# Intermediate stores moved to GpSimd's DMA queue, and the activations for d W2 turned by DMA instead of TensorE

## The chip, the cores and the metric

The kernel runs on one core of one Trainium2 chip. The metric is the device time of one execution in microseconds (us), as a median over runs. A profiled execution, from which every duration below is read, is one more run with its own time.

## What is computed

A gated state-space block, forward and backward in one launch. Sequence length L is 2048, width D 512, state size N 128, hidden width F 1792, all in bf16.

```python
xn = layernorm(x)
s  = ssm_conv(xn)                       # kernel K from A, B, C, dt; FFT convolution over 2L, plus xn * Dskip
g  = silu(silu(xn @ w1) @ w2)           # the dense branch
out = x + s * g
```

The outputs are `out` and, for a given `grad_out`, the gradients of x, of the six real arrays A, B and C (real and imaginary), of log_dt, Dskip, w1 and w2. The gradient of w2 is `silu(h)^T @ d_o`, where `h = xn @ w1` and `d_o` is the gradient at the second product's output. TensorE sums over partitions, so `silu(h)` is needed there with tokens on the partitions. The forward part stores h to DRAM (`Hd`) with the hidden index on the partitions, so it has to be turned.

## The kernel before, in words

**Stages.** (1) Setup: loads, layer norm, tables of sines. (2) Up to about 250 us: `gen_ffn_fwd` runs over eight chunks of 256 tokens, and is paced against a chain of `gen_tables`, `gen_conv_x` and `gen_conv_fwd` for four blocks of 128 channels. (3) `gen_gate_rows` (silu of the dense branch and its slope, in rows) and the last `gen_conv_fwd`. (4) From about 333 to 521 us: `gen_ffn_da` over eight chunks, interleaved with `gen_conv_bwd` for four blocks and with `gen_out`. (5) To the end: `gen_ssm_bwd` (sixteen groups), interleaved with `gen_dw2` followed by `gen_dw1`, and with `gen_ln_bwd`.

**What goes through DRAM.** Stages hand tiles over in DRAM: tables `Ed` (L427) and `Yd` (L438), spectra `Ud` (L500) and `KXd` (L514), the convolution's result `Sd` (L525), the gradients `dUd` (L657), `DHd` (L879) and `Pd` (L888). All of these are stored from the SyncE queue. The hidden `Hd` (L553), `Od` (L563) and the outputs are stored from the GpSimd queue through `k.st`, which is `nc.gpsimd.dma_start`. Nearly all loads, and all turned loads (`dma_start_transpose`), are issued from SyncE; a few small transfers (`Kd`, `dKd`) are issued from ScalarE.

**Names for the steps.** `Kb` (L509) is the convolution kernel read back from `Kd`; `dft_fwd` multiplies by the first DFT matrix (L284), turns the result by DMA (`dB<-dA`, L287), and multiplies by the second (L296, L297); `spectrum_in` (L491) loads a spectrum as `sp_in`; `dft_inv` goes back (L309, L318). `S_b` (L522) is one block of the convolution's result, and `gate_s` (L596) multiplies the gate's `do` by it. `W2T` (L1076) and `W1T` (L857) are the turned weights for the backward products `ps_da` (L874) and `ps_dx` (L885). `doT` (L854) is `do` turned, `slope` (L864) is a load of `Hd`, and `dhT` (L876) is the gradient at h, stored as `DHd`. In the last stage, `load_params` (L345) loads six turned arrays `par_*`; `ssm_fold` loads `GE` (L667) and sums it on TensorE (L683, L685) into `Gf`; `ssm_turned` loads `YT` turned (L705) and `ssm_half` loads `Eb` (L698); `ssm_v` (L716) makes `ps_v`, copied by ScalarE to `Vb`; VectorE multiplies (`Tp`, L726); `ssm_sums` (L738 to L743) adds up `psS` on TensorE. `gen_dw1` loads `dh_tok` turned from `DHd` (L930) and multiplies it with `xn` in blocks of sixteen matmuls (L935). `gen_ln_bwd` loads `du`, `Gt` and `pd_l` (L948, L950, L952).

**d W2.** `gen_dw2` runs over fourteen blocks `ft` of 128 hidden columns. `load(ft)` reads `Hd[ft]` plainly, in rows of 4 KB, into `h_in` (two buffers). `turned` makes sixteen transposes of 128x128 on TensorE into two PSUM tiles, and ScalarE reads each of them through silu into `a_tok` (two buffers). Sixteen matmuls (L917) with `do` follow. Loads run two blocks ahead of the matmuls, turns one block ahead. `gen_dw2` yields sixteen times in all, two of them before its loop.

**What sets the order.** The generators are interleaved by hand-written weights (the last line of the kernel: `[2, 1, 1]`), and a scheduler then sets the order of instructions on each engine and each queue. A queue issues in order: what stands behind a waiting DMA waits too. A tile that takes the place of an earlier one waits for that one's last user.

Of the kernel before, what the change touches and what calls it, by code (L numbers as in the profile page):

```python
# [9 lines left out]
ACT = mybir.ActivationFunctionType  # L10
# [6 lines left out]
P = 128  # L17
# [86 lines left out]
def slope_less_one(nc, u, t):  # L104
# [1 line left out]
    nc.vector.tensor_scalar(out=t, in0=t, scalar1=-0.5, scalar2=0.5, op0=ALU.mult, op1=ALU.add)  # L106
    nc.vector.tensor_single_scalar(out=u, in_=u, scalar=-1.0, op=ALU.add)
    nc.vector.tensor_tensor(out=u, in0=u, in1=t, op=ALU.mult)


def turned(k, src, n, out, ev):

    for i in range(0, n, 8):
        pt = k.pf.tile([P, 8, P], BF16, name="pt_t", tag="pf")
        for j in range(8):
            k.nc.tensor.transpose(out=pt[:, j], in_=src(i + j), identity=k.ident[:])
        ev(out[:, i:i + 8], pt[:])


def run(gen):  # L120
# [275 lines left out]
def gen_tables(k, b):  # L396
# [5 lines left out]
    for h in range(2):  # L402
        hs = slice(b * P + 64 * h, b * P + 64 * h + 64)
        mag = tbl.tile([P, NX, 64], BF16, name="mag", tag="mag")
        nc.sync.dma_start(mag[:].rearrange("p e d -> p (e d)"), k.Md[2 * b + h])
        E = tbl.tile([P, 2, 16, NE, 4], BF16, name="E", tag="E", bufs=2)
        Y = k.Y[h]
        H = tbl.tile([P, 2, 16, 3, 4], BF16, name="H", tag="H")
        qe = lambda ap: ap.rearrange("p e (q a) -> p e q a", a=4)
        for (x0, n) in ((0, 8), (8, 8), (16, 5), (21, 7), (28, 3)):  # L410
            V = tbl.tile([P, 2, 8, 64], I32, name="V", tag="tv", bufs=2)
            TS = nc.vector.tensor_single_scalar
            TT(out=V[:, 1, 0:n], in0=k.tau[:, hs].unsqueeze(1).to_broadcast([P, n, 64]),
               in1=k.ecst[:, x0:x0 + n].unsqueeze(2).to_broadcast([P, n, 64]), op=ALU.mult)
            TS(out=V[:, 0, 0:n], in_=V[:, 1, 0:n], scalar=-float(1 << (PB - 2)), op=ALU.add)
            TS(out=V[:, :, 0:n], in_=V[:, :, 0:n], scalar=32 - PB, op=ALU.logical_shift_left)
            sn = tbl.tile([P, 2, 8, 64], BF16, name="sn", tag="ts", bufs=2)
            nc.scalar.activation(out=sn[:, :, 0:n], in_=V[:, :, 0:n], func=ACT.Sin, scale=-2 * PI_LO / 2.0 ** 32)
            for c in range(2):
                if x0 < NE:  # L420
                    segs = [(E[:, c, :, x0:x0 + n, :], 0, n)]
                else:
                    segs = [(Y[:, c, :, 1:8, :] if x0 == NE else H[:, c], 0, n)]
                for o, s0, s1 in segs:
                    TT(out=o.rearrange("p q e a -> p e q a"), in0=qe(sn[:, c, s0:s1]), in1=qe(mag[:, x0 + s0:x0 + s1, :]), op=ALU.mult)
            yield
        nc.sync.dma_start(k.Ed[b, h], E[:].rearrange("p c q e a -> p (c q e a)"))  # L427
        lo = lambda c: Y[:, c, :, 0:8, :].unsqueeze(2).to_broadcast([P, 16, 3, 8, 4])
        hi = lambda c: H[:, c].unsqueeze(3).to_broadcast([P, 16, 3, 8, 4])
        out = lambda c: Y[:, c, :, 8:32, :].rearrange("p q (k m) a -> p q k m a", m=8)  # L430
        shp = [P, 16, 3, 8, 4]
        for c, (x, y), op in ((0, ((0, 0), (1, 1)), ALU.subtract), (1, ((0, 1), (1, 0)), ALU.add)):
            m1 = tbl.tile(shp, BF16, name="m1", tag="tv", bufs=2)
            m2 = tbl.tile(shp, BF16, name="m2", tag="tm", bufs=1)
            TT(out=m1[:], in0=lo(x[0]), in1=hi(x[1]), op=ALU.mult)
            TT(out=m2[:], in0=lo(y[0]), in1=hi(y[1]), op=ALU.mult)
            TT(out=out(c), in0=m1[:], in1=m2[:], op=op)  # L437
        nc.sync.dma_start(k.Yd[b, h], Y[:].rearrange("p c q j a -> p (c q j a)"))  # L438
        yield
        for q0 in range(0, 16, 8):  # L440
            W = tbl.tile([P, 4, 8, NE, 4], BF16, name="W", tag="W", bufs=2)
            for m, (cm, ec) in enumerate(((0, 0), (1, 1), (2, 1), (1, 0))):
                d0 = hs.start + 4 * q0
                ct = k.CT[:, cm, d0:d0 + 32].rearrange("p (q a) -> p q a", a=4).unsqueeze(2).to_broadcast([P, 8, NE, 4])
                TT(out=W[:, m], in0=E[:, ec, q0:q0 + 8], in1=ct, op=ALU.mult)
            for u in range(2):
                ps = k.pt.tile([P, 4, 84], F32, name="ps_k", tag="pt")
                for q in range(4):
                    for m in range(4):
                        nc.tensor.matmul(out=ps[:, q], lhsT=Y[:, m // 2, q0 + 4 * u + q].rearrange("p j a -> p (j a)"),  # L450
                                         rhs=W[:, m, 4 * u + q].rearrange("p e a -> p (e a)"), start=(m == 0), stop=(m == 3))
                qq = 16 * h + q0 + 4 * u
                k.evk(Xr[:, :, :, qq:qq + 4], ps[:].rearrange("p q (e a) -> p a e q", a=4))
            yield
# [40 lines left out]
def gen_conv_x(k, b):  # L495

    bs = slice(b * P, b * P + P)
    dft = k.dft
    U, _ = yield from dft_fwd(k, dft, lambda t: k.xn[:, t, bs], k.evc)
    k.nc.sync.dma_start(k.Ud[b], U[:].rearrange("p c g k -> p (c g k)"))  # L500
    yield


def gen_conv_fwd(k, b):

    nc, dft = k.nc, k.dft
    bs = slice(b * P, b * P + P)
    Kb = dft.tile([P, 4, 16, 32], BF16, name="Kb", tag="t4")
    nc.sync.dma_start(Kb[:].rearrange("p a t q -> p a (t q)"), k.Kd[b].rearrange("a i (r s) x -> (i r) a (s x)", s=2))  # L509
    for _ in range(LAG):  # L510
        yield
    KX, A2 = yield from dft_fwd(k, dft, lambda t: Kb[:, :, t, :], k.evc)
    U = spectrum_in(k, dft, b, "U")
    nc.sync.dma_start(k.KXd[b], KX[:].rearrange("p c g k -> p (c g k)"))  # L514
    yield
    cplx_mul(k, dft, KX, U)
    S = dft.tile([P, 16, P], BF16, name="S_b", tag="t4")

    def consume(t0, n, ps):
        xd = dft.tile([P, 8, P], BF16, name="xd", tag="cm2")  # L520
        nc.vector.tensor_tensor(out=xd[:], in0=k.xn[:, t0:t0 + n, bs], in1=k.Dbc[:, bs].unsqueeze(1).to_broadcast([P, n, P]), op=ALU.mult)
        nc.vector.tensor_tensor(out=S[:, t0:t0 + n], in0=ps[:], in1=xd[:], op=ALU.add)  # L522
    yield from dft_inv(k, A2, U, k.evc, consume)
    k.S_b = S
    nc.sync.dma_start(k.Sd[b], S[:].rearrange("p t d -> p (t d)"))  # L525
    yield


# [98 lines left out]
def gen_conv_bwd(k, b):  # L627
# [26 lines left out]
        TT(out=xd[:], in0=k.ds[:, t0:t0 + n, bs], in1=k.Dbc[:, bs].unsqueeze(1).to_broadcast([P, n, P]), op=ALU.mult)  # L654
        TT(out=du[:, t0:t0 + n], in0=ps[:], in1=xd[:], op=ALU.add)
    yield from dft_inv(k, A2, KX, k.evc, consume_dx)
    nc.sync.dma_start(k.dUd[b], du[:].rearrange("p t d -> p (t d)"))  # L657
    yield


# [187 lines left out]
def gen_ffn_da(k, da):  # L848
# [3 lines left out]
    for c in range(T // 2):  # L852
# [6 lines left out]
        for f in range(FT // 2):  # L859
# [16 lines left out]
            nc.vector.scalar_tensor_tensor(out=dh[:, i0:i0 + 2, :], in0=dh[:, i0:i0 + 2, :], scalar=1.0, in1=ps[:], op0=ALU.add, op1=ALU.mult)  # L876
            if f in (3, 6):
                f0, n = (0, 8) if f == 3 else (8, 6)
                nc.sync.dma_start(k.DHd[f0:f0 + n, :, 256 * c:256 * c + 256].rearrange("f p n -> p f n"), dh[:, 0:n])  # L879
            yield  # L880
        for t in range(2):
            pd = da.tile([P, D], BF16, name="pd_s", tag="pd_s", bufs=1)
            ps = k.pf.tile([P, D], F32, name="ps_dx", tag="pf")
            for ft in range(FT):
                nc.tensor.matmul(out=ps[:], lhsT=dhs[ft // 8][:, ft % 8, t * P:t * P + P], rhs=k.W1T[:, ft, :],  # L885
                                 start=(ft == 0), stop=(ft == FT - 1))
            k.evb(pd[:], ps[:])
            nc.sync.dma_start(k.Pd[:, 2 * c + t, :], pd[:])  # L888
            yield


def gen_dw2(k, fw):
    nc = k.nc

    def load(ft):
        h = fw.tile([P, k.T, P], BF16, name="h_in", tag="h_in", bufs=2)
        nc.sync.dma_start(h[:].rearrange("p t n -> p (t n)"), k.Hd[ft])
        return h

    def turn(h):  # L900
        a = fw.tile([P, k.T, P], BF16, name="a_tok", tag="a_tok", bufs=2)
        turned(k, lambda t: h[:, t], k.T, a, lambda out, in_: nc.scalar.activation(out=out, in_=in_, func=ACT.Silu))
        return a
    h = load(0)
    yield
    a = turn(h)
    h = load(1)
    yield
    for ft in range(k.FT):
        at = a  # L910
        if ft + 1 < k.FT:
            a = turn(h)
            if ft + 2 < k.FT:
                h = load(ft + 2)
        ps = k.pf.tile([P, k.D], F32, name="ps_w2", tag="pf")
        for t in range(k.T):
            nc.tensor.matmul(out=ps[:], lhsT=at[:, t, :], rhs=k.do[:, t, :], start=(t == 0), stop=(t == k.T - 1))  # L917
        ob = fw.tile([P, k.D], BF16, name="o11", tag="o11", bufs=2)
        k.evb(ob[:], ps[:])
        k.st(k.outs[11][ft * P:ft * P + P, :], ob[:])  # L920
        yield
# [197 lines left out]
```

## Time and profile before

| | |
|---|---|
| median of 3 runs | 766.86 us (765.82 to 766.95) |
| profiled execution: time, span | 765.82 us, 764.0 us |
| mean granted TensorE clock | 0.906 |
| busy PE / PE load / DVE / ACT / POOL | 591.7 / 421.9 / 545.3 / 494.8 / 88.7 us |
| SyncE's DMA queue (q1) | 143.94 MB, 73.2% of the 16 DMA engines |
| GpSimd's DMA queue (q0) | 18.10 MB, 7.0% |
| packets under 512 B | 159921 of 234993 |

How to read the profile: PE is TensorE's matmul stream and PEld its weight loads, which overlap; DVE is VectorE, ACT is ScalarE, POOL is GpSimd, SP is SyncE. "SPq" marks the issue of a DMA on SyncE's queue. The rows of slices cut the span into 40 equal parts and give the busy share in tenths. In a line of waits stand the waiting instruction, what ended the wait, and the total us, count and longest. In a line of the timeline stand start, duration (us), engine, source line, operation, output and input. In a line of stretches stand the stretch, its length, the busy us and count of PE, PE load, DVE, ACT and POOL, then granted clock, DMA share and GB/s.

### The profile page before, as it was taken

How to read it: one execution, taken by the hardware profiler on the slowest of the kernel's cores; microseconds unless marked ns; L12 is line 12 of the kernel's file. 1: busy time of each engine (PE TensorE's matmuls, PEld its weight loads, DVE VectorE, ACT ScalarE, POOL GpSimd, SP SyncE). 2: the span in 40 equal slices, each digit the busy share in tenths (PEclk: the TensorE clock that was granted, in tenths of full speed). 3: DMA queues.
4: the chain of work that ended last, by engine and by line, in shares of the span. 5: the costliest groups of instructions: out<-in, count | busy, mean ns of one | idle time of the engine just before them, and what ended most of it. 6: DMA issues, size and time to landing. Idle time of an engine off the chain costs nothing. (4 is left out here: it accounts for less than half of the span.)

```text
span 764.0 us, 13488 instructions
## 1 busy us (share of the span) xinstructions
PE 591.7 (77%) x5260; PEld 421.9 (55%) x5260; DVE 545.3 (71%) x1110; ACT 494.8 (65%) x692; POOL 88.7 (12%) x167
## 2 busy tenths in 40 slices
PE   0479977898998615668898798993599878899885
PEld 0336663675764413356575475771566646678775
DVE  6979988685987985796786696980353975998500
ACT  5869767788898655475785687740476768864111
POOL 2020110011010352000000000000000013031130
PEclk9979988999999866889999899997599998999998
DMA  9989978499689759999969979235899999766492
GB/s 258 345 174 270 250 220 240 170 248 274 236 215 307 297 166 227 288 296 302 231 211 249 242 220 236 80 114 128 208 217 270 235 312 243 209 139 108 79 189 56
DMA packets 234993, 167.36 MB, mean 219 GB/s; under 512 B 159921, under 2 KB 213169, under 8 KB 231089
## 3 DMA queue, kind: packets, MB, share of 16 engines
q1 hardware_dynamic: 221952, 143.94, 73.2%
q0 software_dynamic: 6224, 18.10, 7.0%
q10 hardware_dynamic: 6752, 4.46, 2.0%
q8 instruction: 41, 0.67, 0.4%
q14 instruction: 24, 0.19, 0.1%
HBM read 65.40 MB, written 62.26 MB: 167 GB/s over the span
## 5 line engine op out<-in xcount | busy, mean ns | idle before, releaser
L42 ACT CAST dA<-ps_s 128x1024 bf16<-128x1024 f32 x96 | 94.3, 1029 | 37.5 <-PE ps_s L297 22.5
L546 PE MATMUL ps_h<-XT,W 128*128 128x256 bf16 x448 | 61.2, 288 | 32.9 <-DMA XT<-xn 26.5
L546 PEld LDWEIGHTS <-W 128*128 128x128 bf16 x448 | 45.4, 103 | 43.4 <-issue 19.6
L726 DVE TENSOR_TENSOR Tp<-Vb,Eb 128x1344 bf16<-128x1344 bf16 x64 | 52.5, 853 | 22.8 <-ACT Vb L42 13.3
L309 PE MATMUL ps_i<-I,sp_in 128*128 128x256 bf16 x384 | 55.9, 296 | 13.6 <-DVE sp_in L332 8.7
L42 ACT CAST dB<-ps_i 128x1024 bf16<-128x1024 f32 x48 | 47.2, 1020 | 29.2 <-PE ps_i L309 23.5
L559 PE MATMUL ps_o<-W,aT 128*128 128x512 bf16 x224 | 58.5, 400 | 3.2 <-ACT aT L552 1.8
L296 PE MATMUL ps_s<-dB,F 128*128 128x512 bf16 x96 | 41.0, 427 | 23.3 <-DMA dB<-dA 20.4
L874 PE MATMUL ps_da<-doT,W2T 128*128 128x256 bf16 x448 | 54.8, 276 | 0.5 <-DVE dhT L876 0.5
L309 PEld LDWEIGHTS <-sp_in 128*128 128x128 bf16 x384 | 38.6, 105 | 29.4 <-DVE sp_in L332 12.6
L935 PE MATMUL ps_w<-dh_tok,xn 128*128 128x256 bf16 x448 | 53.0, 273 | 1.6 <-DMA dh_tok<-DHd 1.6
L885 PE MATMUL ps_dx<-W1T,dhT 128*128 128x512 bf16 x224 | 53.7, 379 | 0.7 <-DVE dhT L876 0.7
L917 PE MATMUL ps_w<-do,a_tok 128*128 128x512 bf16 x224 | 53.9, 390 | 0.0
L874 PEld LDWEIGHTS <-W2T 128*128 128x128 bf16 x448 | 44.2, 99 | 9.3 <-issue 2.5
L42 ACT CAST o<-ps_w 128x256 bf16<-128x256 f32 (+1 forms) x42 | 18.6, 442 | 45.8 <-PE ps_w L935 34.6
L42 ACT CAST Vb<-ps_v 128x672 bf16<-128x672 f32 x64 | 42.6, 723 | 8.7 <-PE ps_v L716 7.3
L935 PEld LDWEIGHTS <-xn 128*128 128x128 bf16 x448 | 42.8, 98 | 7.3 <-issue 2.8
L876 DVE SCALAR_TENSOR_TENSOR dhT<-dhT,ps_da 128x512 bf16<-128x512 bf16 x56 | 37.2, 682 | 12.3 <-PE ps_da L874 11.7
L284 PEld LDWEIGHTS <-TF 128*128 128x128 bf16 x384 | 26.3, 103 | 32.6 <-DMA Kb<-Kd 16.3
L297 PE MATMUL ps_s<-dB,F 128*128 128x512 bf16 x96 | 41.0, 427 | 0.0
L450 PE MATMUL ps_k<-W,Y 128*128 128x84 bf16 x512 | 28.5, 212 | 13.3 <-DVE Y L437 10.2
L450 PEld LDWEIGHTS <-Y 128*128 128x128 bf16 x512 | 25.6, 105 | 23.7 <-DVE Y L437 12.9
(220 smaller groups left out, 1327.1 us busy)
## 6 DMA issues: line engine op xcount, KB each, us to landing
Yd<-Y SPq DMA_DIRECT2D x8, 1024.0 KB, 6.4
sp_in<-Ud SPq DMA_DIRECT2D x8, 1024.0 KB, 7.2
h_in<-Hd SPq DMA_DIRECT2D x14, 512.0 KB, 5.2
Ed<-E SPq DMA_DIRECT2D x8, 672.0 KB, 4.8
Eb<-Ed SPq DMA_DIRECT2D x8, 672.0 KB, 6.1
Hd<-hT POOLq DMA_DIRECT2D x8, 512.0 KB, 6.8
Ud<-dA SPq DMA_DIRECT2D x4, 1024.0 KB, 7.9
KXd<-dA SPq DMA_DIRECT2D x4, 1024.0 KB, 6.1
```

The lines of the kernel that those rows point to most:

```text
L42: return self.nc.scalar.copy(out=out, in_=in_)
L296: nc.tensor.matmul(out=ps[:, 4 * u:4 * u + 4], lhsT=F2[:, m0], rhs=B[:, 0, g0:g0 + 4, :], start=True, stop=False)
L297: nc.tensor.matmul(out=ps[:, 4 * u:4 * u + 4], lhsT=F2[:, m1], rhs=B[:, 1, g0:g0 + 4, :], start=False, stop=True)
L309: nc.tensor.matmul(out=ps[:, g], lhsT=Y[:, c, g0 + g, :], rhs=k.I2[:, c].rearrange("p c m -> p (c m)"), start=(c == 0), stop=(c == 1))
L450: nc.tensor.matmul(out=ps[:, q], lhsT=Y[:, m // 2, q0 + 4 * u + q].rearrange("p j a -> p (j a)"), rhs=W[:, m, 4 * u + q].rearrange("p e a ...
L546: nc.tensor.matmul(out=ps[:, j], lhsT=k.W1[:, dk, ft * P:ft * P + P], rhs=XTv[:, :, dk, :], start=(dk == 0), stop=(dk == DK - 1))
L559: nc.tensor.matmul(out=ps[:], lhsT=aT[:, ft, t * P:t * P + P], rhs=k.W2[:, ft, :], start=(ft == 0), stop=(ft == FT - 1))
L726: k.nc.vector.tensor_tensor(out=Tp[:, c, :, r ^ c].rearrange("p e (q w) a -> p q w e a", w=2), in0=Vb[:, :, c].rearrange("p q w (e a) -> p ...
L874: nc.tensor.matmul(out=ps[:, j], lhsT=W2T[:, dk, ft * P:ft * P + P], rhs=dTv[:, :, dk, :], start=(dk == 0), stop=(dk == DK - 1))
L885: nc.tensor.matmul(out=ps[:], lhsT=dhs[ft // 8][:, ft % 8, t * P:t * P + P], rhs=k.W1T[:, ft, :], start=(ft == 0), stop=(ft == FT - 1))
L917: nc.tensor.matmul(out=ps[:], lhsT=at[:, t, :], rhs=k.do[:, t, :], start=(t == 0), stop=(t == k.T - 1))
L935: nc.tensor.matmul(out=ps[:], lhsT=k.xn[:, t, dk * P:dk * P + P], rhs=dh[:, t].rearrange("p j n -> p (j n)"), start=(t == 0), stop=(t == k ...
```

## The change

Two things change. Eight lines that stored `Ed`, `Yd`, `Ud`, `KXd`, `Sd`, `dUd`, `DHd` and `Pd` through `nc.sync.dma_start` call `k.st` instead, so that these 64 DMAs are issued from GpSimd's queue. And `gen_dw2` loads `Hd[ft]` with a turning DMA straight into `a_tok` and applies silu there in place, in one ScalarE instruction of 128x2048; `turned`, `load` and `h_in` go away, as do the two yields before the loop. The scheduler then sets a new order on all engines.

```diff
-        nc.sync.dma_start(k.Ed[b, h], E[:].rearrange("p c q e a -> p (c q e a)"))
+        k.st(k.Ed[b, h], E[:].rearrange("p c q e a -> p (c q e a)"))
...
-        nc.sync.dma_start(k.Yd[b, h], Y[:].rearrange("p c q j a -> p (c q j a)"))
+        k.st(k.Yd[b, h], Y[:].rearrange("p c q j a -> p (c q j a)"))
...
-    k.nc.sync.dma_start(k.Ud[b], U[:].rearrange("p c g k -> p (c g k)"))
+    k.st(k.Ud[b], U[:].rearrange("p c g k -> p (c g k)"))
...
-    nc.sync.dma_start(k.KXd[b], KX[:].rearrange("p c g k -> p (c g k)"))
+    k.st(k.KXd[b], KX[:].rearrange("p c g k -> p (c g k)"))
...
-    nc.sync.dma_start(k.Sd[b], S[:].rearrange("p t d -> p (t d)"))
+    k.st(k.Sd[b], S[:].rearrange("p t d -> p (t d)"))
...
-    nc.sync.dma_start(k.dUd[b], du[:].rearrange("p t d -> p (t d)"))
+    k.st(k.dUd[b], du[:].rearrange("p t d -> p (t d)"))
...
-                nc.sync.dma_start(k.DHd[f0:f0 + n, :, 256 * c:256 * c + 256].rearrange("f p n -> p f n"), dh[:, 0:n])
+                k.st(k.DHd[f0:f0 + n, :, 256 * c:256 * c + 256].rearrange("f p n -> p f n"), dh[:, 0:n])
...
-            nc.sync.dma_start(k.Pd[:, 2 * c + t, :], pd[:])
+            k.st(k.Pd[:, 2 * c + t, :], pd[:])
...
 def gen_dw2(k, fw):
     nc = k.nc
-
-    def load(ft):
-        h = fw.tile([P, k.T, P], BF16, name="h_in", tag="h_in", bufs=2)
-        nc.sync.dma_start(h[:].rearrange("p t n -> p (t n)"), k.Hd[ft])
-        return h
-
-    def turn(h):
+    for ft in range(k.FT):
         a = fw.tile([P, k.T, P], BF16, name="a_tok", tag="a_tok", bufs=2)
-        turned(k, lambda t: h[:, t], k.T, a, lambda out, in_: nc.scalar.activation(out=out, in_=in_, func=ACT.Silu))
-        return a
-    h = load(0)
-    yield
-    a = turn(h)
-    h = load(1)
-    yield
-    for ft in range(k.FT):
-        at = a
-        if ft + 1 < k.FT:
-            a = turn(h)
-            if ft + 2 < k.FT:
-                h = load(ft + 2)
+        nc.sync.dma_start_transpose(a[:], k.Hd[ft])
+        nc.scalar.activation(out=a[:], in_=a[:], func=ACT.Silu)
         ps = k.pf.tile([P, k.D], F32, name="ps_w2", tag="pf")
         for t in range(k.T):
-            nc.tensor.matmul(out=ps[:], lhsT=at[:, t, :], rhs=k.do[:, t, :], start=(t == 0), stop=(t == k.T - 1))
+            nc.tensor.matmul(out=ps[:], lhsT=a[:, t, :], rhs=k.do[:, t, :], start=(t == 0), stop=(t == k.T - 1))
```

More of the change, by code (lines that the diff above doesn't have):

```diff
@@ L108, in slope_less_one @@
     nc.vector.tensor_tensor(out=u, in0=u, in1=t, op=ALU.mult)
[L111 to L117, printed above, removed]
 def run(gen):
```

## The prediction

> **What bounds the kernel now.** I read the 40 slices first, then busy times by stage, the SyncE queue in order of time, and single tiles. In the slices, PE and DMA share the load and no engine is full everywhere.
>
> ```profile
> PE   0479977898998615668898798993599878899885
> DMA  9989978499689759999969979235899999766492
> ```
>
> Two holes in PE stand out: at 269 to 285 us, and at 522 to 546 us. The longest PE waits name them:
>
> ```profile
> PE ps_s L284 <- DMA Kb<-Kd: 16.2, 1, 16.2
> PE G L683 <- DMA GE<-dKd: 14.7, 1, 14.7
> ```
>
> The SyncE queue tells why the first is long. The load of Kb (L509) stands behind a store of S_b that waits for VectorE until 275.85 and a load of G that waits until 279.43:
>
> ```profile
> 269.29 0.33 SPq L575 DMA_DIRECT2D G<-in_grad_out_dram  x1
> 275.85 0.33 SPq L525 DMA_DIRECT2D Sd<-S_b  x1
> 279.43 0.33 SPq L575 DMA_DIRECT2D G<-in_grad_out_dram  x1
> 279.93 0.38 SPq L509 DMA_DIRECT2D Kb<-Kd  x1
> 280.41 10.13 SPq L1076 DMA_TRANSPOSE W2T<-in_B_w_dram  x4
> 291.73 6.40 SPq L287 DMA_TRANSPOSE dB<-dA  x1
> ```
>
> The second hole is the chain par, GE, fold: the queue reaches the six parameter loads at 522.74, and GE, behind them, at 530.45:
>
> ```profile
> 522.74 1.17 SPq L345 DMA_TRANSPOSE par_Ar<-in_A_A_re_dram  x1
> 530.45 2.66 SPq L667 DMA_DIRECT2D GE<-dKd  x4
> ```
>
> The d W2 stage (first load of h_in at 541.9 to the last at 645.9) shows busy us of PE, PE load, DVE, ACT, POOL, then clock and DMA share:
>
> ```profile
> 541.90:645.90 104.00, 88.22 (x876) 63.89 (x877) 65.52 (x149) 72.89 (x115) 11.28 (x21) 0.90 1.02 252
> 716.00:757.00 41.00, 36.18 (x325) 30.66 (x323) 10.14 (x39) 8.14 (x21) 7.13 (x12) 1.00 0.67 136
> ```
>
> A DMA share of 1.02 over 104 us (packets of one engine overlap, so it can pass 1) says that the DMA engines pace it, with PE (85%) close. From 716 only d W1 is left and PE runs through: 20 blocks of 16 matmuls by 755.9, 2.02 us each; 8.1 us of last store and end follow.
>
> **What the Trainium skill says.** "DMA: Bandwidth & Descriptors", section "Issuing engines are not separate DMA queues", says that all issuers share the same 16 DMA engines and another issuer saves sequencer time only. The trace fits: a 512 KB store from GpSimd (Hd) lands in 6.8 us, a load of that size from SyncE (slope) in 5.1. "SBUF — State Buffer", section "SBUF: two separate sides", warns that VectorE's fast modes can keep GpSimd from writing descriptors. Here all 16 Hd issues took 828 to 2342 ns, median 864, beside a VectorE over 80% busy: no such block to speak of. "Advanced Engine Details and Errata", section "X-Bar Transpose (TRN2)", calls turned DMAs as fast as plain ones. This trace disagrees: turned loads move in packets of 256 B at 25 ns on average, plain 4 KB rows in packets at 202 ns (packet records), so 512 KB takes 2048 x 25 / 16 = 3.2 us of all 16 engines against 128 x 202 / 16 = 1.6 us.
>
> **The change part by part.** The sum is against the profiled execution, 765.82 us (span 764.0), and stands 1.04 us below the median of 766.86.
>
> *1. Stores to GpSimd.* 64 issues leave SyncE: 8 Ed, 8 Yd, 4 each of Ud, KXd, Sd and dUd, 16 DHd, 16 Pd. A SyncE issue is about 0.35 us, 64 x 0.35 = 22 us of a queue that is not full; GpSimd gains 64 x 0.6 = 38 us and was busy 12%. Cost in bytes: none. Up to 250 us the built order differs little, and the turned loads dB start when their data is ready, not behind a store: 0, with +-4 for the new order. On GpSimd stores now stand among the gate's tensor_scalars, but VectorE needs S_b there in the same order: 0.
>
> *2. 269 to 366 us.* Kd lands about 274.5, the store and the fourth G load no longer stand before Kb: it goes at 274.5 instead of 279.9, a gain of 5.5 us. But in the built order W1T (issue 11.7 us in this trace, 8.7 at best) now stands before both dB, and W2T before it. From 274.5: four W2T, 9 to 10 us; G, S, S, 1.5; W1T, 10 to 11; so dB goes at 297 where it now goes at 291.7, and lands at 305.5 (now 299.9). The U load for the same product comes after the second dB: issue 309, landing 315.5 (now 304.85). The first ps_da, now at 333.3, then starts near 338: +5. W1T is out of the way and the slopes are ready by then, which takes back about 2 of the PE gaps of 2.9 and 3.6 us at 338 and 351: net +3.
>
> *3. 366 to 521 us.* Loads no longer wait behind DHd, Pd and dUd, whose waits on SyncE sum to 20.8, 22.8 and 10.8 us; but PE itself waits only 5.9 us (418 us), 2.6 and 2.8 for dB here. I take back 3, bounds 0 and 8.
>
> *4. The boundary.* SyncE's order is now: two a_tok, eight loads of the layer norm's backward and three dh_tok, all ahead of par and GE. The first dh_tok waits for the last DHd store of the first eight rows (VectorE at 514.5, landing near 519), each takes 2.4 to 3 us of issue, and loads of du, Gt and pd_l between them wait for buffers until about 525. So par goes at 529 instead of 522.7: +6.5 for GE. PE fills the hole with two d W2 blocks (32 x 0.213 = 6.8 us). The first ps_v, which now stands after the h_in wait (landing 546), comes at 543.7 + 6.5 = 550.2, not 546.5.
>
> *5. d W2.* Removed: 224 turns on PE, 0.059 us apart in the rows of 16, 13.2 us; 28 ScalarE silus x 1.03 = 28.9 us, replaced by 14 of 128x2048, 1.92 each (row dhT L865) = 26.9 us. Added: 14 turned loads for 14 plain ones, (3.2 - 1.6) x 14 = 22 us of the 16 engines.
>
> ```profile
> L897 SPq DMA_DIRECT2D h_in<-Hd x14: 319/512/977, 541.9 to 645.9; - x14
> L930 SPq DMA_TRANSPOSE dh_tok<-DHd x14: 1317/3008/6394, 594.7 to 742.5; - x14
> h_in<-Hd SPq DMA_DIRECT2D x14, 512.0 KB, 5.2
> dh_tok<-DHd SPq DMA_TRANSPOSE x14, 6.5
> ```
>
> (The first two: issue time in ns, least, median, most; the others: us to landing.) Two a_tok, three dh_tok and eight loads left the stage (part 4). Packets of 537 to 646 sum to 112 us over 16; by the same prices, Eb 11, YT 36, GE 7, twelve a_tok 39, one dh_tok 3, eleven small loads 10, stores 12, scaled by 112/117, the new stage has 113. It starts at 543, four later. The old depth, two h_in and two a_tok, shrinks to two a_tok, each loaded only after the matmuls of two blocks before: I take 1.00 instead of 1.03 of the engines. The last a_tok goes at 656; 8 us landing (dh_tok: 5.1 to 10.2), 1.9 silu, 4.5 wait and matmuls end d W2 at 670.4. The third block starts near 567, after the fourth ps_v as the built order has it, so a pair of blocks takes (670.4 - 567) / 6 = 17.2 us.
>
> *6. The tail.* At that point the order leaves eight groups of psS (2.4 us), six of ps_v (1.15), ten d W1 blocks (1.75) and the rest, 44.4 us of PE work; the old stretch from 672.5 to 715.5 took 1.19 times its work: 52.8 us. Then 18 d W1 blocks, not 20: 36.4 us, and 8.1. End: 670.4 + 97.3 = 767.7 of span, +3.7.
>
> Sum: +3 - 3 + 3.7 = +3.7, 769.5 profiled, **770.5** as a median.
>
> **The rivals.** Everything hangs on the pair's time p: the end moves by 6p - 99.7 us, break-even p = 16.6.
> *Faster:* the d W2 stage is paced by PE, not by DMA. Then the 13.2 us of turns and 6.8 us put in the hole count in full. p = 15 gives 6 x 15 - 99.7 = -9.7, 757. For it: PE 19.6 of 20 us at 560 to 600; floor of p: 6.5 landing + 1.9 + 3.6 = 12. Against: the share of 1.02 to 1.08. It decides below 16.6.
> *Much slower:* the loop of load, silu and matmul holds SyncE, with YT queued behind an a_tok that waits for PE, and ScalarE, where Vb stands behind a silu that waits for DMA. p = 20 gives +20, 787. For it: SyncE and ScalarE keep their order; against: the two loads of a pair overlap.
> *Nothing to be seen:* stores change the queue's name only, 112 against 113 us of packets, p near 16.6: 767.
>
> **How the numbers follow.** The likeliest, +1.5 to +12: 0.38; much slower: 0.17; faster: 0.34; nothing: 0.11. A measurement here tells 0.2% (1.5 us) from no change. Slower is 0.38 + 0.17 = 0.55. The range reaches from p near 14.2, 752, to p near 20.2, 788; the likeliest's own is 768 to 779.
>
> **What would show it.** Kb issued near 274 and the first dB near 297; ps_da first near 338; par near 529; two d W2 blocks at 522; last d W2 matmul near 670; DMA share near 1.0 in the stage; 18 d W1 blocks after the last psS. If the last d W2 matmul comes before 660, I am wrong towards faster; if ScalarE stands long before the a_tok silus, towards slower.

## The result, and the profile after

The changed kernel takes 791.49 us (median of 4, 790.96 to 794.53), the kernel before 766.34 beside it: a ratio of 1.0352, 95% interval 1.0299 to 1.0405, so 3 to 4% slower. The forecast was 770.5, and the time lies above its range of 752 to 788. The profiled execution of the changed kernel took 790.96 us, span 789.2 (before 764.0): 25.2 us to be found. Beside the experiments the kernel before has medians of 760 to 764, so from here on ratios are compared. In the tables below "us" is the median of all runs, while the ratio leaves out runs more than 1.5% above their kernel's fastest, as the profiled executions of e1, e3, e13 and e14 were, so that for e1, e3 and e14 the traces of their repetitions e16, e18 and e17 are read, and of e13 only the order at the boundary. All points in time are those of one profiled execution.

The slices, from the page of the changed kernel:

```profile
PE   0589876897988623478799398899178866799887
DMA  9997868599479789988849949568899989958564
```

The hole at 270 us has become shallower and longer (2, 3, 4 from 276 to 335 us), a new one (3) stands at 434 to 454 us, and that at the boundary is deeper (1). From the waits of PE: who waited, for what, total us, times, longest.

```profile
PE ps_s L287 <- DMA dB<-dA: 36.8, 7, 12.6
PE ps_s L275 <- ACT dA L42: 16.9, 5, 8.2
PE G L674 <- DMA GE<-dKd: 16.6, 1, 16.6
PE ps_s L275 <- DMA Kb<-Kd: 7.4, 1, 7.4
```

As forecast, the wait for Kb has shrunk (16.2 before) and that for GE has not. The wait for dB has grown from 20.4 us to 36.8, that for ScalarE's dA from 6.4 to 16.9. The two lines of before:

```profile
PE ps_s L296 <- DMA dB<-dA: 20.4, 7, 5.9
PE ps_s L284 <- ACT dA L42: 6.4, 6, 5.2
```

SyncE's queue, in order of time:

```profile
276.74 0.33 SPq L566 DMA_DIRECT2D G<-in_grad_out_dram  x1
277.24 0.38 SPq L500 DMA_DIRECT2D Kb<-Kd  x1
277.79 10.89 SPq L1050 DMA_TRANSPOSE W2T<-in_B_w_dram  x4
292.94 0.33 SPq L566 DMA_DIRECT2D G<-in_grad_out_dram  x1
293.32 0.91 SPq L593 DMA_DIRECT2D S<-Sd  x2
294.27 9.69 SPq L848 DMA_TRANSPOSE W1T<-in_B_w_dram  x1
304.07 10.03 SPq L278 DMA_TRANSPOSE dB<-dA  x2
...
519.09 7.61 SPq L887 DMA_TRANSPOSE a_tok<-Hd  x2
532.52 0.37 SPq L922 DMA_DIRECT2D du<-dUd  x1
...
542.78 2.07 SPq L904 DMA_TRANSPOSE dh_tok<-DHd  x1
...
545.53 3.52 SPq L904 DMA_TRANSPOSE dh_tok<-DHd  x1
...
550.68 3.56 SPq L904 DMA_TRANSPOSE dh_tok<-DHd  x1
554.29 1.28 SPq L336 DMA_TRANSPOSE par_Ar<-in_A_A_re_dram  x1
...
562.17 2.65 SPq L658 DMA_DIRECT2D GE<-dKd  x4
```

Two things are to be seen. W1T stands before both dB, which go at 304.07 (before 291.73); and the fourth G load stands behind the four W2T, at 292.94 (before 279.43, ahead of them). At the boundary par stands behind loads that wait for stores to land: du for the last dUd store (landed 532.38), the first dh_tok for a DHd store (landed 542.65). SyncE stands for 5.8 and 7.4 us there, with par behind. The two stores on GpSimd, with GpSimd's own wait in brackets:

```profile
529.43 0.56 POOL L648 DMA_DIRECT2D dUd<-du_b  x1 [3.49 <-DVE du_b L646]
537.15 0.90 POOL L870 DMA_DIRECT2D DHd<-dhT  x1 [2.24 <-DVE dhT L867]
```

The last stage, first a_tok load behind the boundary to the last, and then d W1 alone (busy us of PE, PE load, DVE, ACT, POOL; clock, DMA share):

```profile
584.86:676.68 91.82, 70.46 (x593) 45.13 (x591) 48.44 (x110) 57.27 (x77) 9.61 (x18) 0.91 0.97 200
747.50:783.80 36.30, 33.00 (x297) 27.84 (x294) 10.12 (x39) 7.34 (x19) 6.79 (x11) 1.00 0.57 122
```

The queues and landings (the rows of q1 and q0: packets, MB, share of 16 engines; the others: size, us to landing):

```profile
q1 hardware_dynamic: 227552, 108.03, 60.3%
q0 software_dynamic: 13648, 54.01, 19.7%
...
a_tok<-Hd SPq DMA_TRANSPOSE x14, 6.9
```

Where the 25 us came from, as ends of the same work in us (par: issue):

| | before | after | later by |
|---|---|---|---|
| forward stage, last ps_o | 241.3 | 248.4 | 7.1 |
| last S_b | 322.4 | 342.9 | 20.5 |
| last ps_dx | 521.6 | 544.3 | 22.7 |
| par_Ar goes | 522.7 | 554.3 | 31.6 |
| first G | 541.4 | 572.9 | 31.5 |
| last d W2 matmul | 672.5 | 693.8 | 21.3 |
| last psS | 715.6 | 747.5 | 31.9 |
| last d W1 matmul | 755.9 | 783.8 | 27.9 |

So 22.7 us are there before the last stage begins, 8.8 come at the boundary, and what follows takes back 6.3.

### The profile page after: what moved, and what is told of

Its sections match the earlier page's. It is cut to its first block, busy times and chain, and to the rows that moved or that the text cites. A ratio compares the mean times of both kernels' runs of the same rounds, so it can differ in the third digit from the quotient of the medians.

```text
span 789.2 us, 13075 instructions
## 1 busy us (share of the span) xinstructions
PE 587.1 (74%) x5036; PEld 408.0 (52%) x5036; DVE 547.1 (69%) x1110; ACT 493.3 (63%) x678; POOL 129.4 (16%) x231
## 3 DMA queue, kind: packets, MB, share of 16 engines
q1 hardware_dynamic: 227552, 108.03, 60.3%
q0 software_dynamic: 13648, 54.01, 19.7%
## 4 chain that ended last, share of the span: by engine, by line
issue 29%; DVE 18%; DMA 18%; PE 17%; ACT 7%; POOL 6%; SPq 4%; POOLq 0%; ACTq 0%; DVEq 0%
DMA dB<-dA 4%; DMA a_tok<-Hd 4%; PE ps_dx L876 3%; DVE Tp L717 2%; PE ps_w L891 2%; DMA G<-in_grad_out_dram 2%; PE ps_i L300 2%; PE ps_da L865 2%; SPq L904 1%; POOL Hd L544 1%; DMA slope<-Hd 1%; PE ps_o L550 1%; DMA Od<-ob 1%; DMA out_dram<-go_x 1%; DVE g_t L751 1%
## 5 line engine op out<-in xcount | busy, mean ns | idle before, releaser
L42 ACT CAST dA<-ps_s 128x1024 bf16<-128x1024 f32 x96 | 94.5, 1028 | 56.2 <-PE ps_s L288 40.4
L287 PE MATMUL ps_s<-dB,F 128*128 128x512 bf16 x96 | 42.2, 440 | 39.5 <-DMA dB<-dA 36.8
L891 PE MATMUL ps_w<-do,a_tok 128*128 128x512 bf16 x224 | 57.4, 408 | 16.7 <-ACT a_tok L888 16.7
L42 ACT CAST dB<-ps_i 128x1024 bf16<-128x1024 f32 x48 | 47.3, 1024 | 24.4 <-PE ps_i L300 20.2
L909 PE MATMUL ps_w<-dh_tok,xn 128*128 128x256 bf16 x448 | 53.7, 273 | 1.2 <-DMA dh_tok<-DHd 0.7
L320 DVE TENSOR_TENSOR cm<-sp_in,dA 128x1024 bf16<-128x1024 bf16 x24 | 16.5, 689 | 47.8 <-ACT dA L42 31.8
L891 PEld LDWEIGHTS <-a_tok 128*128 128x128 bf16 x224 | 22.1, 103 | 43.8 <-ACT a_tok L888 18.2
L42 ACT CAST o<-ps_w 128x256 bf16<-128x256 f32 (+1 forms) x42 | 18.5, 439 | 40.9 <-PE ps_w L909 32.3
L888 ACT ACTIVATE a_tok<-a_tok 128x2048 bf16<-128x2048 bf16 x14 | 26.6, 1910 | 27.1 <-DMA a_tok<-Hd 27.1
L288 PE MATMUL ps_s<-dB,F 128*128 128x512 bf16 x96 | 41.6, 433 | 0.0
```

Source lines behind the costliest of these rows:

```text
L42: return self.nc.scalar.copy(out=out, in_=in_)
L287: nc.tensor.matmul(out=ps[:, 4 * u:4 * u + 4], lhsT=F2[:, m0], rhs=B[:, 0, g0:g0 + 4, :], start=True, stop=False)
L288: nc.tensor.matmul(out=ps[:, 4 * u:4 * u + 4], lhsT=F2[:, m1], rhs=B[:, 1, g0:g0 + 4, :], start=False, stop=True)
L891: nc.tensor.matmul(out=ps[:], lhsT=a[:, t, :], rhs=k.do[:, t, :], start=(t == 0), stop=(t == k.T - 1))
L909: nc.tensor.matmul(out=ps[:], lhsT=k.xn[:, t, dk * P:dk * P + P], rhs=dh[:, t].rearrange("p j n -> p (j n)"), start=(t == 0), stop=(t == k ...
```

## Experiments

### One part at a time: e1 to e4, e16, e18

e1 has all 64 stores on GpSimd and the old d W2; e2 the new d W2 and the old stores; e3 only the forward stores (Ed, Yd, Ud, KXd, Sd); e4 only the backward stores (dUd, DHd, Pd). e16 and e18 are e1 and e3 once more. The edit of e4, for one of its three lines:

```diff
-            nc.sync.dma_start(k.Pd[:, 2 * c + t, :], pd[:])
+            k.st(k.Pd[:, 2 * c + t, :], pd[:])
```

> All eight kinds of store (64 DMAs) from GpSimd's queue, d W2 as before. Theory A, drawn from the trace after: the moved stores alone, by the order that the scheduler then builds, cost nearly everything: the last ps_dx ends near 544 (before 521.6), and the time is 785 to 791. Theory B, the prediction on record: moved stores cost nothing up to the boundary: last ps_dx within 4 us of 521.6, time 763 to 770.

> Only d W2 changed (turned by DMA, silu in place); all stores from SyncE as before. Theory A: up to 521 us nothing moves (the built order is the same until there), and the d W2 stage and its tail cost +2 to +6: 768 to 773. Rival (much slower loop, p near 20): 785 to 790. Rival (PE-paced, p 15): near 757.

> Only the five forward stores (Ed, Yd, Ud, KXd, Sd; 28 DMAs) from GpSimd, d W2 as before. In its built order W1T already stands before both dB of the last forward convolution. Theory A (the order of loads in the forward part and in the last convolution is the cause): most of the +22, 780 to 788, first ps_da chunk ends near 358. Theory C (each issue on GpSimd costs its share, whichever it is): 28/64 of +22, near 776. Theory B: 763 to 770.

> Only the three backward stores (dUd, DHd, Pd; 36 DMAs) from GpSimd, d W2 as before; W1T stays behind both dB in its built order. Theory A: little, 763 to 770, first ps_da chunk near 349. Theory C (each issue on GpSimd costs its share): 36/64 of +22, near 779.

> The kernel of e1 once more, since the profiled execution of e1 was the longest of its 20 runs (779.5 us against a median of 770.4). Theory A: the order is the same, so the last S_b comes again near 341 and the last ps_dx 530 to 544; par goes 16 to 18 us ahead of the last ps_dx, as with backward stores alone; time 765 to 773. Rival (a part of the delay in e1's profile was chance): S_b below 335.

> The kernel of e3 once more, since its profiled execution was among the longer of its runs. Theory A: the last S_b again near 342 and Kb near 277, since both follow from the order; time 771 to 779. Rival: S_b below 335.

| | us | ratio to before (95%) | last ps_o | last S_b | last ps_dx | par goes | first G |
|---|---|---|---|---|---|---|---|
| e1 | 770.4 | 1.0063 (1.0030 to 1.0097) | | | | | |
| e16 | 764.4, one run | before 762.6 | 246.7 | 341.5 | 540.2 | 523.8 | 546.3 |
| e2 | 766.9 | 1.0042 (1.0015 to 1.0069) | 241.8 | 320.9 | 519.7 | 530.4 | 550.2 |
| e3 | 776.4 | 1.0143 (1.0111 to 1.0176) | | | | | |
| e18 | 778.2, one run | before 762.6 | 246.7 | 342.1 | 535.6 | 536.6 | 555.2 |
| e4 | 747.2 | 0.9782 (0.9719 to 0.9844) | 240.9 | 321.3 | 521.4 | 504.6 | 527.3 |

The delay of the forward stage and of S_b belongs to the forward stores: e18 has it whole, e4 and e2 not at all. Theory C (a price for each issue on GpSimd) falls with e4: 36 of the 64 issues, and no delay. Theory A was wrong on the times of e1, e3 and e4: e3's 776.4 is the figure of theory C, below A's 780 to 788, and e4 gains 2.2%, at the boundary. e2 came out near the lower end of its theory A: 2.8 us above the kernel before, expected +2 to +6. The timeline of SyncE in e4:

```profile
495.46 0.36 SPq L864 DMA_DIRECT2D slope<-Hd  x1
504.60 1.16 SPq L345 DMA_TRANSPOSE par_Ar<-in_A_A_re_dram  x1
...
512.61 2.66 SPq L667 DMA_DIRECT2D GE<-dKd  x4
```

Before, nine stores that wait for VectorE and ScalarE stand between the slope load at 499.59 and par at 522.74. With these on GpSimd, par goes 16.8 us ahead of the last ps_dx, and the first G ends 5.9 us behind it instead of 19.8. e16 shows the same (16.4 and 6.1), and so e1 pays back most of its forward loss.

The two parts don't add up: e1 and e2 alone lose 0.6% and 0.4%, together 3.5%. What the stores gain at the boundary is missing in the changed kernel, where par goes 10.0 us behind the last ps_dx. Nor do the two groups of stores add up: the forward ones cost 1.4% alone (e3), 2.9% where the backward ones are moved as well (e1 against e4, 1.0063 / 0.9782), and 3.5% in the changed kernel (1.0352 / 1.0006, e7 below). One place where they meet can be seen. PE's longest wait for dB between 400 and 460 us is 5.9 us before, 4.5 in e4 and 6.2 in e18, but 10.2 in e16 and 12.6 in the changed kernel. No run takes that wait out by itself, so how much of the difference it makes is open.

### The boundary: e6, e7, e8, e13, e15

e7 is the changed kernel with the forward stores back on SyncE. e6 is the changed kernel, and e13 is e7, with the first du, pd_l and dh_tok made to wait for par, so that par and GE go first; e15 is e13 with a third a_tok buffer. e8 joins e6 to the edit of e5 below. Each copy makes the load behind it wait:

```diff
+    k.p1c = par["Ci"][:, 0:1]
...
+        if c < 2:
+            nc.gpsimd.tensor_copy(du[:, 0, 0, 0:1], k.p1c)
         nc.sync.dma_start(du[:].rearrange("p b t d -> p b (t d)"), k.dUd[:, :, 256 * c:256 * c + 256].rearrange("b p n -> p b n"))
...
+        if c < 2:
+            nc.gpsimd.tensor_copy(pd[:, 0, 0:1], k.p1c)
         nc.sync.dma_start(pd[:], k.Pd[:, 2 * c:2 * c + 2, :])
...
+            if f < 2:
+                nc.gpsimd.tensor_copy(dh[:, 0, j, 0:1], k.p1c)
             nc.sync.dma_start_transpose(dh[:, :, j, :], k.DHd[2 * f + j])
```

```diff
-        a = fw.tile([P, k.T, P], BF16, name="a_tok", tag="a_tok", bufs=2)
+        a = fw.tile([P, k.T, P], BF16, name="a_tok", tag="a_tok", bufs=3)
```

> The changed kernel, but the first loads of du, pd_l and dh_tok made to wait for the last par load (one column of par is copied into their tiles ahead of the load), so that par and GE go out before them. Theory A (par stands behind loads that wait for stores to land, and the gain that backward stores alone had is lost there): par goes at 527 to 530 instead of 554, first G ends near 551 (changed kernel 572.6), and the time falls by 15 to 22: 769 to 776. Rival (the last stage is paced by the DMA engines, so an earlier G is given back in the d W2 stage): first G as above but time 784 to 790.

> The changed kernel, but the five forward stores back on SyncE: backward stores on GpSimd and d W2 turned by DMA. Theory A (the two parts work against each other at the boundary: the turned loads bring du and dh_tok ahead of par, where they wait for stores): the 17 us that backward stores alone gained are lost, first G near 550, time 766 to 772. Rival (the parts add up: -17 and +3): 748 to 753.

> The changed kernel with both edits: W1T behind both dB, and par and GE ahead of du, pd_l and dh_tok. Theory A: the two gains add, 755 to 763, the +7 of the forward stage remains in it. Rival (one shared limit, the DMA engines or PE, takes one of the two back): 768 to 776.

> As e7 (backward stores on GpSimd, d W2 turned by DMA), with par and GE ahead of the first du, pd_l and dh_tok, as in e6. Theory A (turning by DMA costs nothing by itself; its price is the place of par in the queue): par goes near 505, first G ends near 530 with two d W2 blocks ahead of it, and the time falls from e7's ratio of 1.00 to about 0.98, as with backward stores alone. Rival (the turned loads and their silu slow the d W2 stage itself, so an earlier G is given back there): par near 505 but ratio 0.995 to 1.005.

> As e13, with a third buffer for a_tok. Theory A (with two buffers each load waits for the matmuls of two blocks before, and PE for load and silu: gaps of 3 to 8 us ahead of a_tok blocks): these gaps shrink and the time falls by 3 to 8 us below e13. Rival (the DMA engines pace the stage): within 3 us of e13, or slower since more turned loads stand ahead of YT.

| | us | ratio to before (95%) | par against last ps_dx | first G behind last ps_dx |
|---|---|---|---|---|
| before | | 1 | +1.1 | 19.8 |
| after | 791.5 | 1.0352 (1.0299 to 1.0405) | +10.0 | 28.6 |
| e7 | 760.6 | 1.0006 (0.9980 to 1.0031) | +10.8 | 29.5 |
| e6 | 772.7 | 1.0172 (1.0077 to 1.0268) | -17.9 | 10.5 |
| e8 | 769.5 | 1.0111 (1.0034 to 1.0189) | -18.5 | 10.5 |
| e13 | 750.2 | 0.9847 (0.9817 to 0.9877) | -17.7 | 10.5 |
| e15 | 746.6 | 0.9820 (0.9758 to 0.9882) | -16.8 | 5.9 |

From the timeline of e7: the first dh_tok waits, and par stands behind the third.

```profile
509.50 0.38 SPq L926 DMA_DIRECT2D pd_l<-Pd  x1
517.45 1.36 SPq L904 DMA_TRANSPOSE dh_tok<-DHd  x1
...
525.27 4.28 SPq L904 DMA_TRANSPOSE dh_tok<-DHd  x1
529.59 1.26 SPq L336 DMA_TRANSPOSE par_Ar<-in_A_A_re_dram  x1
```

From the timeline of e6, where nothing that waits for a store is left ahead of par:

```profile
521.90 7.96 SPq L888 DMA_TRANSPOSE a_tok<-Hd  x2
529.91 1.05 SPq L929 DMA_DIRECT2D Gt<-in_grad_out_dram  x2
531.05 1.15 SPq L336 DMA_TRANSPOSE par_Ar<-in_A_A_re_dram  x1
```

Theory A holds for e6 and e13, and for e7 by the ratio; the 760.6 us of e7 lie between the two ranges, since the kernel before stood at 760.1 there. Had the parts been additive, e7 would have had 0.9782 x 1.0042 = 0.982; it has 1.0006. With par first it has 0.985 (e13): of the 2.2 points that e7 lost against e4, 1.6 come back. The rest, 0.65 points, isn't clear of the two intervals, which overlap. So most of the price of the turned load was par's place in the queue, and what it costs as such can't be told from nothing here. The rival of e6 (an earlier G given back in the d W2 stage) falls by the median, which drops by 1.8 points of the ratio. G came at 559.5 and not at 551, since in that execution (780.5 us, the longest of e6's four) the last ps_dx ended at 549.0; part is given back, though: G is 13.4 us earlier than in the changed kernel, the last d W1 matmul 10.5. Its PE waits:

```profile
PE ps_w L892 <- ACT a_tok L889: 25.6, 9, 7.0
```

and that of e15, with three buffers:

```profile
PE ps_w L892 <- ACT a_tok L889: 4.9, 3, 2.5
```

The wait for load and silu is real, 25.6 us in e6, and with a third buffer it is 4.9 (e15). The buffer isn't shown to be the cause, though, for it changed the order as well. The first a_tok loads of e13 (first line) stand ahead of par, at 507.33; those of e15 (second line) stand behind par, at 502.19, and behind GE and four YT:

```profile
498.60 5.29 SPq L888 DMA_TRANSPOSE a_tok<-Hd  x2
523.61 5.42 SPq L888 DMA_TRANSPOSE a_tok<-Hd  x2
```

In time e15 and e13 aren't told apart: their intervals overlap. e8 has 1.0111, where the sum of both gains would give 1.0352 - 0.0133 (e5) - 0.0180 (e6) = 1.0039. That is just inside its interval, but its 769.5 us lie in the range of the rival (768 to 776) and not in that of theory A (755 to 763): whether the two gains add in full is not shown.

### The last convolution and the forward stage: e5, e9, e10, e11, e14, e17

e5 is the changed kernel with W1T made to wait for the first half of the last S_b; e9 adds a third buffer for G, so that its fourth load needn't wait:

```diff
+            nc.gpsimd.tensor_copy(k.W1T[:, 0, 0:1], k.S_b[:, 0, 0:1])
             nc.sync.dma_start_transpose(k.W1T[:], k.ins["B_w1"])
```

```diff
-        G = gp.tile([P, 4, k.D], BF16, name="G", tag="G", bufs=2)
+        G = gp.tile([P, 4, k.D], BF16, name="G", tag="G", bufs=3)
```

e10 is the kernel before with only Ed and Yd on GpSimd, e11 with only Ud, KXd and Sd (lines as in e4). e14 is the changed kernel with the edits of e5, e9 and e6, and Ed and Yd back on SyncE; e17 is e14 once more.

> The changed kernel, but the load of W1T made to wait for the first half of the last S_b (one column of S_b is copied into W1T ahead of the load), so that both dB of the last forward convolution go out before it. Theory A (W1T ahead of dB costs stage 3): the last S_b comes near 329 to 331 (changed kernel 342.9, before 322.4; the rest of the delay is there before W1T), and all later points 11 to 14 us earlier: 777 to 781, ratio to before about 1.017. Rival (the delay of stage 3 comes from the stores' landing or from ScalarE's order): S_b stays near 340, time 788 to 792.

> The changed kernel with W1T behind both dB (as in e5), and a third buffer for G, so that the fourth G load goes out ahead of Kb and the four W2T and not behind them. Theory A (two orders on SyncE make up the delay of the last convolution: W1T ahead of dB, and the last G behind W2T, for which the gate, ds and the second product wait): the PE gap of 8 us at 297 goes, the last S_b comes at 324 to 328 (e5: 334.6, changed kernel 342.9), and the time is 768 to 775 where the kernel before has 764. Rival (the gap of 8 us is ScalarE's own order): S_b stays within 2 us of e5's 334.6, time as e5, about 1.02 of the kernel before.

> Only the stores of Ed and Yd (16 DMAs) from GpSimd, all else as before; W1T stays behind both dB, but the order of PE changes from the same place on as with all forward stores. Theory A (the +7 of the forward stage comes from the new order of work on PE, which these two stores set off): ps_o ends near 247 (before 241.3), time 769 to 774. Rival (the spectra's stores, which spectrum loads and dB stand behind, cause it): ps_o near 241, 763 to 767.

> Only the stores of Ud, KXd and Sd (12 DMAs) from GpSimd, all else as before; W1T stays behind both dB. Theory A (see e10): ps_o ends within 2 us of 241.3, Kb goes about 3 to 5 us earlier, since Sd no longer stands before it, time 759 to 765. Rival: ps_o near 247, time 769 to 774.

> The changed kernel with W1T behind both dB, a third buffer for G, par and GE first, and the stores of Ed and Yd back on SyncE. Theory A (four places in the order explain all of it): the delay of the forward stage falls to 2 or 3, the last S_b comes near 326, and the ratio to before is 0.99 to 1.005. Rival (a part of the loss lies in the stores' queue itself or elsewhere): 1.01 or more, as e8 (1.011).

> The kernel of e14 once more, since in e14's profiled execution (775.1 us against a median of 765.4) one turned dB took 22.8 us to land. Theory A: ps_o ends near 244, the last S_b near 327, time 760 to 767. Rival (putting the tables' stores back does nothing for the forward stage): ps_o near 247 and S_b near 331, as in e9.

| | us | ratio to before (95%) | last ps_o | first dB | last S_b | S_b behind ps_o |
|---|---|---|---|---|---|---|
| before | | 1 | 241.3 | 291.7 | 322.4 | 81.1 |
| after | 791.5 | 1.0352 (1.0299 to 1.0405) | 248.4 | 304.1 | 342.9 | 94.5 |
| e5 | 778.2 | 1.0219 (1.0133 to 1.0306) | 246.4 | 296.7 | 334.6 | 88.2 |
| e9 | 771.3 | 1.0161 (1.0075 to 1.0247) | 247.0 | 298.6 | 331.3 | 84.3 |
| e10 | 762.6 | 1.0048 (1.0023 to 1.0073) | 246.7 | 299.4 | 329.5 | 82.8 |
| e11 | 766.6 | 1.0069 (1.0035 to 1.0102) | 243.7 | 293.2 | 326.8 | 83.1 |
| e14 | 765.4 | 1.0047 (1.0017 to 1.0077) | | | | |
| e17 | 766.0, one run | before 762.6 | 244.3 | 293.5 | 333.3 | 89.0 |

The timeline of e5 answers to that of the changed kernel: dB no longer has W1T ahead of it.

```profile
293.34 0.33 SPq L566 DMA_DIRECT2D G<-in_grad_out_dram  x1
293.71 0.91 SPq L593 DMA_DIRECT2D S<-Sd  x2
294.67 0.43 SPq L856 DMA_DIRECT2D slope<-Hd  x1
296.66 6.49 SPq L278 DMA_TRANSPOSE dB<-dA  x1
```

S_b comes 8.3 us earlier; 2.0 of them are there at ps_o already, so that W1T's place is worth 6.3, less than the 12 to 14 expected. (From the last ps_o to the last S_b the five traces read with the forward stores on SyncE take 79.1 to 82.2 us, the four with all of these moved and W1T ahead of dB 93.1 to 95.3, and e8, which has the edit of e5, 87.3.) The hole of 12.6 us at 437 is gone in e5 as well, yet the last ps_dx comes only 9.3 us earlier. W1T's new place has a price of its own: doT now stands behind W1T (332.34), and the first ps_da waits for it.

```profile
PE ps_da L866 <- DMA doT<-do: 6.3, 1, 6.3
```

The rest of the 13.0 us by which the span falls comes in the last stage. The hole, in the changed kernel's timeline of SyncE:

```profile
422.59 0.33 SPq L605 DMA_DIRECT2D go_g<-Od  x1
432.20 0.33 SPq L610 DMA_DIRECT2D go_x<-in_A_u_dram  x1
...
433.10 7.42 SPq L278 DMA_TRANSPOSE dB<-dA  x1
```

go_x waits 9.3 us for a store of the output (GpSimd 423.26) to land at 432.18, and dB behind it. e16 has it too (10.2 us), e5 and e9 don't: there the same loads meet at other times.

The second order, G behind W2T, gives back 3.9 us, counted from ps_o (e9). The wait of 8 us for dA that it was to explain is still 7.0, so theory A fell for that part. What dA waits for is the end of the gate's work on VectorE: 304.34 in the changed kernel, and the cast starts at 304.42 (before 294.96 and 295.04). The gate begins late, as the forward stage before it is late: the first ds starts at 269.3, not 262.1. And in the changed kernel the 8 us don't count in full, since the first dB lands only at 311.0.

The forward stage's 7 us: the tables alone give 5.4 (e10), the spectra alone 2.4 (e11), so that theory A has the larger part right. In the stretch from 100 to 250 us PE waits 7.2 us for dB before, 12.5 in e10, 11.4 in e16. In time both expectations fell: e10 costs 0.5%, less than expected, and e11 0.7%, where next to nothing was expected. Putting the tables back does bring ps_o to 244.3 (e17), as theory A said, but S_b comes at 333.3, not at 327, near what its rival said: there PE waits 7.5 us for casts of dB on ScalarE, which stand behind a silu that waits 8.7 us for its slope load. In all these kernels W1T goes late, at 328 to 332 us (e5, e9, e17). With all four edits the median is 765.4, ratio 1.0047, at the edge of theory A's range, beside e8's 1.0111; the intervals overlap, and S_b doesn't bear theory A out. Nor is 1 the right mark for it. e13 has the same backward stores, d W2 and edit at the boundary, with all forward stores on SyncE, and reaches 0.9847. So with Ud, KXd and Sd on GpSimd about 2 points (1.0047 against 0.9847) are still missing after both edits for the last convolution, more than the 0.7% of these stores alone (e11): the four places don't explain all of the loss.

### A faster version: e4, e12

> A version meant to be faster than both: the kernel before with dUd, DHd, Pd and Sd stored from GpSimd and a third buffer for G, d W2 by TensorE as before. Theory A (what helps is what takes a waiting DMA from ahead of a load that PE waits for: Pd and DHd ahead of par, Sd and the fourth G ahead of Kb): Kb goes near 275 (before 279.9), par near 500 (before 522.7), and it is 3 to 6 us faster than backward stores alone, 741 to 745, ratio to before about 0.974. Rival (Kb earlier is taken back by W2T and dB behind it): as backward stores alone, ratio 0.978 to 0.982.

e12 moves dUd, DHd, Pd and Sd and gives G a third buffer: 747.5 us, ratio 0.9858 (0.9758 to 0.9957). Kb goes at 271.8 and par at 493.9, but the time is that of e4 (0.9782), within the intervals: theory A's 741 to 745 fell, and nothing gained beyond e4 can be shown. The backward stores alone beat both kernels by what the runs can tell: e4's interval is a gain of 1.6 to 2.8% over the kernel before. So do e13 and e15, whose intervals reach from 1.2 to 2.4%.

## Why the prediction was wrong

The forecast of +3.7 us in span became +25.2. By its own steps:

**Step 1 failed:** "Up to 250 us ... 0, with +-4 for the new order." It is +7.1. (The last ps_o ends at 239.8 to 242.9 in the five traces read with the forward stores on SyncE, and at 245.7 to 249.7 in the seven with all of these moved.) I had seen that the order changes and priced it by the queue's load. The stores were no load; moving them changed the order of everything else.

**Step 2 failed in size:** "net +3" for 269 to 366 us. From the forward stage to the last S_b it is +13.4. The mechanism was named: Kb early (277.2, forecast 274), W1T ahead of dB (304.1, forecast 297). I followed dB along SyncE, though, and let the start of the stretch stand where it was. The fourth G load stood in my own list behind the four W2T, and I didn't ask who waits for it: the gate, then dA, then PE, which keeps its order (8.2 us). Of the 13.4 us, the edit to W1T's place gives back 6.3 and that to G's 3.9, though G's didn't take away the wait it was meant for; 3.2 are left. A term that the sum didn't have is TensorE's clock. Between the last ps_o and the last S_b PE is busy for 45.0 us where it was 39.6 before, on nearly as many matmuls, and the granted clock is 0.66 instead of 0.75 (before, then the changed kernel):

```profile
241.30:322.40 81.10, 39.60 (x321) 26.75 (x321) 63.92 (x89) 45.13 (x60) 20.68 (x17) 0.75 0.87 255
248.40:342.90 94.50, 45.00 (x319) 29.64 (x320) 65.73 (x87) 52.41 (x65) 23.82 (x22) 0.66 0.92 273
```

In e9 it is 39.7 us at 0.72. So the 3.2 us, and a part of what the two edits gave back, may be the clock's; no run tests it.

**Step 3 failed too:** "I take back 3, bounds 0 and 8" became +2.2, counted from the last S_b to the last ps_dx, with a wait in it that the trace of before had at 5.9 us and that became 12.6. Where step 2 ends and step 3 begins depends on the mark. The first ps_da, forecast near 338, starts at 346.7, which is 13.4 late; the ps_dx of its chunk end at 372.8 instead of 364.4, only 8.4 late, so that by this mark nearly all of step 2's loss moves to step 3. The products of dB in gen_conv_bwd, between which these chunks run, stay late all the while: the second starts at 393.9 (before 373.3), the third at 449.3 (before 423.9). The waits on SyncE that I summed for step 3 (20.8, 22.8, 10.8) are those of the whole run; from 366 to 521 us they are 15.3, 20.2 and 6.7.

**Step 4** erred by 2.4 us: first ps_v 31.0 us behind the last ps_dx, forecast 28.6. What I named was there: two a_tok, the layer norm's loads and three dh_tok ahead of par, two d W2 blocks in the hole. What I did not see is that the moved stores alone take par 18 us forward (e4). In the changed kernel that gain is hidden by the loads that the second part puts there, so the two parts were worth -2.2% (backward stores) and +0.4%, and together 0.06% (e7).

**Steps 5 and 6 held in their sums.** The third block starts at 594.6, 27.6 late against 567 (22.7 from above, 5 from the boundary), and from there the pair takes (693.8 - 594.6) / 6 = 16.5 us (forecast 17.2); the tail takes 53.7 + 36.3 + 5.4 = 95.4 (forecast 97.3). Together 6.1 less than forecast, and 27.6 - 6.1 = 21.5 is the whole error in span. The rivals' disputed quantity was p, and it came out at the break-even of 16.6: **the sum was argued over the stage that hardly moved.** What paces that stage is not shown: its DMA share is 0.97 (forecast 1.00), and PE waits 16.7 us there for a_tok, whose silus wait 27.1 us for their loads on ScalarE. That is the sign I gave for "much slower", and the wait is there, but with p at 16.5, not 20, and the new d W2 alone costs 0.4% (e2). "Much slower" had nearly the right time by luck: the loss lay elsewhere.

**The Trainium skill.** "DMA: Bandwidth & Descriptors", section "Issuing engines are not separate DMA queues", holds: the moved 35.9 MB leave q1 and arrive on q0 at about the same price. q0 grew from 7.0% of 764.0 to 19.7% of 789.2 us, by 102 us of 16 engines; q1 fell from 73.2% to 60.3%, by 83 us, with an estimated 22 us of turned loads added (step 5), so by 105. A forecast that stops at that sentence gives 0 for step 1, as mine did. The warning in "SBUF — State Buffer", section "SBUF: two separate sides", isn't seen here either: 16 DHd issues took 836 to 937 ns. "Advanced Engine Details and Errata", section "X-Bar Transpose (TRN2)", against which I charged the 22 us: a_tok lands in 6.9 us where h_in took 5.2, and yet e13 isn't slower than e4 by more than their intervals. No run shows a loss of time from the turned loads as such.

**Left open:** why the order of e17 keeps S_b at 333 with the forward stage nearly mended, where the 2 points between e14 and e13 go, and how much of the forward stage's delay is the place of the loads, and how much PE's and ScalarE's new order. A move of the stores with every other order held was not tried. The mean granted clock is 0.906 before, 0.893 in the changed kernel and 0.925 in e4; whether it follows the holes in PE or adds to the time by itself wasn't tested.

## What to carry to other kernels

Where a scheduler sets the order, a moved DMA is an edit to all queues: list each load that comes to stand elsewhere, and for each ask what it waits for, what stands behind it and which engine waits for that. A store that waits is worth moving off the queue whose next load opens a stage (here 2.2% for three stores), but loads that wait for those same stores to land must not take the place. Test two edits apart as well as together: here the gain of one was hidden by the other.

## What the runs showed of the hardware

The moved stores of up to 672 KB landed later from GpSimd's queue in the changed kernel than from SyncE's before, as medians: the 128 KB Pd in 3.7 us instead of 2.8, DHd of 384 KB in 5.3 instead of 3.8, Sd (512 KB) in 4.5 instead of 3.2. Of those of 1 MB, Yd took 6.4 in both, and KXd 4.8 instead of 6.1. What else the DMA engines carried at these moments differs between the two, so the queue isn't shown as the cause. du and dh_tok wait for such a landing. A turned load holds SyncE for long: a_tok of 512 KB took 2.0 to 4.8 us to issue, h_in of the same size 0.3 to 1.0.
